# Stage-one blocks from GpSimd sums in a Fourier mixer and MLP on one NeuronCore

## The chip, the cores and the metric

One core of a Trainium2 chip runs the whole kernel in one launch. Its engines are TensorE (PE, with its weight loads shown as PEld), VectorE (DVE), ScalarE (ACT), GpSimd (POOL) and SyncE (SP), which here only issues DMAs. The metric is the device time of one execution in microseconds; the median of the runs counts.

## The reference

```python
B, S, D, FF = 8, 3008, 256, 2048            # batches, sequence, width, hidden width
X = np.fft.rfft(x, axis=1)                  # along the 3008 rows of each batch
Yr = X.real @ w_r - X.imag @ w_i + b_r
Yi = X.real @ w_i + X.imag @ w_r + b_i
Y = shrink(Yr, 0.01) + 1j * shrink(Yi, 0.01)   # sign(v) * max(|v| - 0.01, 0)
y = np.fft.irfft(Y, n=3008, axis=1).reshape(B * S, D)
out = np.maximum(y @ w_in, 0) ** 2 @ w_out  # 24064 tokens, 256 -> 2048 -> 256
```

## The kernel before

The transform over 3008 = 64 x 47 rows is done in two stages each way, by products with constant matrices. **Stage one** of a batch is 13 blocks (q = 0 to 12) of 120 partitions. A block is loaded as xt, which holds two halves of 2 x 256 columns; the host has laid row g beside its mirror row, so that the sum of the two halves goes through the cosine matrix am and their difference through the sine matrix. There are two ways to do a block. `Fwd` lets GpSimd make sum and difference (xs, two operations of line 215) and TensorE multiply each once (two products of line 236). `Fwd2` leaves GpSimd out: it multiplies both halves and lets the accumulator add them, with nam, the negative of the sine matrix, for the second half of the difference (four products of line 352). Either way ScalarE copies the result out of the accumulator psf into xe, and a DMA stores it to s in DRAM. **Stage two** (`Pair`, 12 a batch) reads two groups of all 13 blocks back (ka) with their matrices (kb), multiplies them (line 280), splits the result into a high and a low part (kxh by ScalarE, kxl by VectorE or GpSimd) and mixes it with the complex weights (line 301); shrink and the first inverse stage follow. The second inverse stage (`Back`: loads du, products of lines 461, 464 and 465, results yr) gives the tokens of the MLP.

**The MLP** runs in 48 tiles of 500 or 504 tokens (six to a batch), each in eight steps. A step does its first layer by seven products of half blocks, each as three passes of high and low parts (line 484, accumulators psh), in place of eight; VectorE puts the accumulators together (mp, mu, mv, mc), ScalarE applies relu and square and rounds to the high part of mg, GpSimd subtracts to get the low part, and TensorE multiplies by wout into pso. The operands of the seven products are sums of the tile's tokens (yt), made by VectorE for tile 0 and by GpSimd from tile 1 on. The MLP's weights come as 64-bit words in 16 parts; their conversion (dst, da, df, dw and then win or wout, lines 148 to 163) runs before the main part for 13 of them and for the last three inside it, at the half steps m = 1, 3 and 5 (`LATER`).

Batch 0 and blocks 0 to 4 of batch 1 (`PRE = 5`) are done in the front part. The main part then runs a loop over half steps m. In its first 16 the remaining eight blocks of batch 1, q = 5 to 12, are put between the steps of tile 0, at m of 0.5 + 0.9 (q - 5). The first `Pair` of batch 1 comes at 11.2, where tile 1's inverse stage is done too. Batch 2's blocks, by `Fwd`, start at 14.6.

What sets the order: the numbers beside each job give the order in which the program is recorded; a scheduler then orders each engine's instructions by its own model of times. `then` holds TensorE, VectorE, ScalarE and GpSimd to the recorded order for the steps' own operations, `load_next` does so for the loads on SP's queue. Tiles have 2 buffers where the tables say nothing; psf has two banks, xs, xe and du one buffer. The memory of the conversion is given up behind m = 5, and the tiles named in `SIDE` (xs among them) move there. nam is made twice, once for the front part and once for the main part (lines 712 and 713).

Of the kernel before, what the change touches and what calls it, by code (L numbers as in the profile page):

```python
# [9 lines left out]
F32 = mybir.dt.float32  # L10
# [13 lines left out]
B, S, D, FF = 8, 3008, 256, 2048  # L24
# [3 lines left out]
R, J = 5, 13  # L28
M1 = R * G
# [8 lines left out]
}  # L38
MAIN = {
    "xs": 1, "xe": 1, "du": 1, "kv": 1, "kp": 1, "kq": 1, "ksh": 1, "ksl": 1, "kxl": 1, "kb": 1, "yr": 1,  # L40
    "ms": 1, "mp": 1, "mu": 1, "mv": 1, "mc": 3, "nam": 1,
}
CONV = ("big", "small", "dw", "ds")
SIDE = ("xs", "ka", "kb", "kcm", "kxh", "kxl", "kp", "kq", "ke", "kv", "ksh", "ksl", "kuh", "kul", "ku")

# [11 lines left out]
def fnet_moe(ctx: ExitStack, tc, x, w_r, w_i, b_r, b_i, w_in, w_out, bm, cm, dx, a32, c32, out):  # L59
    nc = tc.nc  # L60
# [278 lines left out]
    class Fwd2(Fwd):  # L339
# [2 lines left out]
            with tc.issue_after(after.ins):  # L342
                nc.sync.dma_start(self.xt, x[self.b, :, self.q:self.q + 1])

        def add(self):
            pass

        def run(self):
            ps = bank([128, 2, D])
            for t in range(2):  # L350
                for i in range(2):
                    nc.tensor.matmul(
                        ps[:M1, t], nam if t and i else am32[:, t], self.xt[:, 0, i], start=i == 0, stop=i == 1
                    )
            self.ev = T("xe", [M1, 1, 2, D], F32, tag="xe" if self.q >= PRE else "xf")
            copy(act, self.ev[:, 0], ps[:M1])
            self.store(nc.sync if self.q >= PRE else act)

# [305 lines left out]
    PRE = 5  # L666
    nam = T("nam", [M1, M1], F32)
    act.mul(nam, am32[:, 1], -1.0)
    second = [Fwd2(1, q) for q in range(J)]
    for r in range(-5, len(units) + 3):  # L670
        at(units, r + 5, "load")
        at(units, r + 1, "fwd", "bins")
# [36 lines left out]
            chain[nc.sync] = p.get  # L709
    for n in range(len(parts) - LATE, min(LATER.values())):  # L710
        convert(n, units[-1])
    nam = T("nam", [M1, M1], F32)
    act.mul(nam, am32[:, 1], -1.0)
    for q in range(PRE, PRE + 2):
        second[q].load()
    jobs = []
    for m in range(2 * len(steps) + 4):
        b, r = divmod(m, slots)
        if r == 0 and b < B:
            jobs = [(t - slots, job) for t, job in jobs]  # L720
            if b + 1 < B:
                first, step, end = 1.0, 6.1, 7.1
                if b == 0:
                    first, step, end = 11.2, 5.3, 9.1
                    for q in range(PRE, J):
                        if q > PRE + 1:
                            jobs += [(0.9 * (q - PRE - 2), second[q].load)]
                        jobs += [(0.5 + 0.9 * (q - PRE), second[q].run)]
                    jobs += [(first - 0.6, pairs[1][0].load)]
                jobs += pair_tasks(pairs[b + 1], first, step, end)  # L730
            if b + 2 < B:
                first, step = (2.6, 7.0) if b else (14.6, 6.0)
                jobs += fwd_tasks(b + 2, first, step) + [(95.0, pairs[b + 2][0].load)]
            for j in range(len(HALF)):
                t = b * len(HALF) + j + 1
                if t < len(tiles):
                    jobs += back_tasks(t, NF * j + 0.5)
            jobs.sort(key=lambda j: j[0])
        n, k = divmod(m, 2)
        if k and 0 <= n - 2 < len(steps):  # L740
            steps[n - 2].out(1)
        if n < len(steps):
            (steps[n].second if k else steps[n].first)()
        if not k and 0 <= n - 2 < len(steps):
            steps[n - 2].out(0)
        if m in LATER:
            convert(LATER[m], steps[n])
        if m == max(LATER):
            conv.close()
            pools.update(dict.fromkeys(CONV), **dict.fromkeys(SIDE, memory(ctx, "side")))  # L750
        while jobs and jobs[0][0] < r + 1:
            jobs.pop(0)[1]()
# [86 lines left out]
```

## Time and profile before

| | us |
|---|---|
| runs of the kernel before | 2613.71, 2615.43, 2618.53 |
| their median | 2615.43 |
| the profiled execution | 2614.82 |
| its span in the trace | 2613.1 |
| TensorE busy in it | 2564.3 |
| VectorE, ScalarE, GpSimd busy | 1782.3, 1672.7, 1657.0 |

The profile gives one execution: the busy time of each engine, the same by stretches of time, each instruction with what ended the idle time ahead of it, and the waits that each engine had. A share over the whole span is an average of stages: the front part, where the weights are converted and batch 0 is transformed, ends at about 126 us; the change lies behind it.

### The profile page before, as it was taken

To read this page: it belongs to the slowest core of one execution; us is meant where nothing else is said; L and a number is where in the kernel's file an instruction comes from. 1 tells how busy PE (TensorE), PEld (TensorE's weight loads), DVE (VectorE), ACT (ScalarE), POOL (GpSimd) and SP (SyncE) were. 2 spreads that over 40 slices of the span, in tenths; PEclk is the share of its full clock that TensorE was granted. 3 is DMA by queue.
4 is the path that set the end of the run, shared out by engine and by line. 5 is a ranking of instruction groups with operands and counts; after the bars stand their busy time and mean duration, and the time that the engine had idled before them with its cause. 6 is when DMAs were issued, how large, how long until landed. Compare 5 with 4: busy or idle time off the path is not lost.

```text
span 2613.1 us, 47540 instructions
## 1 busy us (share of the span) xinstructions
PE 2564.3 (98%) x16908; PEld 2347.0 (90%) x16908; DVE 1782.3 (68%) x3797; ACT 1672.7 (64%) x2434; POOL 1657.0 (63%) x1628
## 2 busy tenths in 40 slices
PE   6799999999999999999999999999999999999999
PEld 4689989999999999999999999999999999999998
DVE  6877766667767767577676776667676677765554
ACT  3556656666666666666666666666666666666665
POOL 2246666766766667667666676666667666666564
PEclk8999999999999999999999999999999999999999
DMA  8733332333332332233332333323332223221100
GB/s 267 236 110 110 102 113 82 95 106 107 95 91 75 116 104 86 84 95 113 104 92 82 97 110 100 99 76 101 103 108 80 71 79 101 71 65 41 33 17 17
DMA packets 191455, 250.51 MB, mean 96 GB/s; under 512 B 21755, under 2 KB 135923, under 8 KB 191219
## 3 DMA queue, kind: packets, MB, share of 16 engines
q1 hardware_dynamic: 178240, 223.89, 28.1%
q0 software_dynamic: 12304, 22.35, 3.6%
q8 instruction: 136, 2.23, 0.4%
q10 hardware_dynamic: 675, 1.23, 0.2%
q14 instruction: 100, 0.82, 0.1%
HBM read 146.85 MB, written 100.53 MB: 95 GB/s over the span
## 4 chain that ended last, share of the span: by engine, by line
PE 84%; POOL 1%; DMA 1%; issue 0%; DVE 0%; ACT 0%; POOLq 0%; SPq 0%; ACTq 0%; DVEq 0%
PE pso L484 36%; PE psh L484 32%; PE psf L301 6%; PE psf L280 2%; PE psf L236 2%; PE psf L333 2%; PE psf L464 1%; PE psf L465 1%; PE psf L461 1%; DMA du<-s 1%; POOL mg L101 0%; POOL yt L101 0%; POOL ms L101 0%; POOL ms L500 0%; ACT mc L484 0%
## 5 line engine op out<-in xcount | busy, mean ns | idle before, releaser
L101 POOL TENSOR_TENSOR mg<-mc,mg 128x500 fp32r<-128x500 f32 (+1 forms) x768 | 975.0, 1290 | 594.3 <-ACT mg L97 549.7
L484 PE MATMUL pso<-mg,wout 128*128 128x500 f32 (+1 forms) x4608 | 1176.2, 392 | 1.8 <-ACT mg L97 1.3
L484 PE MATMUL psh<-yt,win 128*128 128x250 f32 (+1 forms) x8064 | 1072.9, 281 | 1.5 <-DVE mc L484 1.2
L484 ACT ACTIVATE mc<-mc 128x1000 f32<-128x1000 f32 (+1 forms) x768 | 802.6, 1045 | 406.6 <-DVE mc L484 397.3
L484 PEld LDWEIGHTS psh<-yt,win 128*128 128x128 f32 x8064 | 1022.2, 189 | 34.3 <-PE psh L484 1.9
L484 PEld LDWEIGHTS pso<-mg,wout 128*128 128x128 f32 x4608 | 818.7, 189 | 130.0 <-POOL mg L101 1.9
L484 DVE TENSOR_TENSOR mc<-psh,mv 128x500 f32<-128x500 f32 (+3 forms) x768 | 419.1, 547 | 428.1 <-PE psh L484 395.4
L97 ACT CAST mg<-mc 128x1000 fp32r<-128x1000 f32 (+1 forms) x384 | 396.9, 1034 | 18.4 <-ACT mc L484 0.4
L484 DVE TENSOR_TENSOR mv<-psh,mu 128x500 f32<-128x500 f32 (+1 forms) x384 | 260.6, 679 | 53.5 <-PE psh L484 21.8
L301 PE MATMUL psf<-wx,kxh 128*128 128x256 f32 x1008 | 206.7, 281 | 2.4 <-ACT kxh L97 1.7
L98 DVE COPY mp<-psh 128x250 f32<-128x250 f32 (+1 forms) x384 | 159.7, 416 | 39.2 <-PE psh L484 16.2
L301 PEld LDWEIGHTS psf<-wx,kxh 128*128 128x128 f32 x1008 | 166.3, 189 | 6.7 <-ACT kxh L97 1.9
L101 POOL TENSOR_TENSOR ksl<-kv,ksh 128x512 fp32r<-128x512 f32 x84 | 108.8, 1295 | 94.6 <-ACT ksh L97 94.5
L484 DVE TENSOR_TENSOR mu<-psh,mp 128x250 f32<-128x250 f32 (+1 forms) x384 | 160.5, 418 | 11.5
L215 POOL TENSOR_TENSOR xs<-xt 120x256 f32<-120x256 f32 x156 | 115.4, 760 | 72.5 <-DMA xt<-x_in 67.6
L484 DVE TENSOR_TENSOR mc<-psh,mp 128x250 f32<-128x250 f32 (+1 forms) x384 | 156.8, 408 | 4.3 <-PE psh L484 2.8
L322 DVE TENSOR_TENSOR kv<-psf,ke 64x256 f32<-64x256 f32 x336 | 141.8, 422 | 22.9 <-PE psf L301 14.2
L301 PE MATMUL psf<-wx,kxl 128*128 128x256 f32 x504 | 141.1, 280 | 1.0 <-DVE kxl L101 1.0
L97 ACT COPY dy<-psf 128x188 f32<-128x188 f32 x256 | 76.9, 313 | 82.7 <-PE psf L465 82.2
L313 DVE TENSOR_TENSOR ke<-psf,bias 128x512 f32<-128x512 f32 x84 | 58.0, 691 | 102.0 <-PE psf L301 101.9
L97 ACT CAST ksh<-kv 128x512 fp32r<-128x512 f32 x84 | 52.0, 619 | 114.3 <-DVE kv L101 113.4
L97 ACT CAST kuh<-psf 128x256 fp32r<-128x256 f32 x192 | 68.4, 372 | 88.2 <-PE psf L333 71.4
(102 smaller groups left out, 2565.4 us busy)
## 6 DMA issues: line engine op xcount, KB each, us to landing
du<-s SPq DMA_DIRECT2D x128, 256.0 KB, 2.9
s<-kuh SPq DMA_DIRECT2D x192, 128.0 KB, 1.8
s<-kul SPq DMA_DIRECT2D x192, 128.0 KB, 1.8
kcm<-cm_in POOLq DMA_DIRECT2D x84, 256.0 KB, 3.3
ka<-s SPq DMA_DIRECT2D x84, 256.0 KB, 3.4
s<-xe SPq DMA_DIRECT2D x87, 240.0 KB, 2.4
xt<-x_in SPq DMA_DIRECT2D x86, 240.0 KB, 3.3
du<-s SPq DMA_DIRECT2D x256, 64.0 KB, 2.8
```

What stands on the lines that cost most here:

```text
L97: return act.copy(out=out, in_=in_)
L98: return eng.tensor_copy(out=out, in_=in_)
L101: return eng.tensor_tensor(out=out, in0=a, in1=b, op=ALU.subtract)
L215: return eng.tensor_tensor(out=out[:, :n], in0=self.xt[:, :n, 0], in1=self.xt[:, :n, 1], op=(ALU.add, ALU.subtract)[t])
L236: nc.tensor.matmul(ps[:M1, t], am32[:, t], self.u[:, t], start=True, stop=True)
L280: nc.tensor.matmul(pv[:, :, c, g, :], self.a[:, g, c * 128:(c + 1) * 128], bg, start=True, stop=True)
L301: self.last = nc.tensor.matmul(ps, l, wx[j][:, k, c, :], start=n == 0, stop=n == 5)
L313: dve.tensor_add(out=self.e, in0=self.pe, in1=bias)
L322: dve.tensor_add(out=v[64 * r:64 * r + 64, g], in0=ps[gs], in1=self.e[gs, r])
L333: nc.tensor.matmul(ps[:, :D], self.cm[:, g, j * 128:(j + 1) * 128], r[:, g], start=n == 0, stop=n == 2)
L461: mm = nc.tensor.matmul(pv[:, :, 0], self.u[:, 0, cs], dx_sb[:, 0], start=True, stop=False)
L484: last_of[eng] = op(*args, **kwargs)
```

## The change

The eight blocks q = 5 to 12 of batch 1 are done by `Fwd` in place of `Fwd2`. Each gets a job `add` (two GpSimd operations, xs from xt) 0.6 of a half step ahead of its job `run`, which issues two products in place of four. The second nam and its ScalarE operation go; xs lies in the main memory from the start, and no longer in the one that is opened behind m = 5. The evacuation tile and the queue of the stores stay what they were for these blocks (xe, SP); `Fwd2`, now for the front part alone, loses the choice.

```diff
 MAIN = {
-    "ms": 1, "mp": 1, "mu": 1, "mv": 1, "mc": 3, "nam": 1,
+    "ms": 1, "mp": 1, "mu": 1, "mv": 1, "mc": 3,
 }
-SIDE = ("xs", "ka", "kb", "kcm", "kxh", "kxl", "kp", "kq", "ke", "kv", "ksh", "ksl", "kuh", "kul", "ku")
+SIDE = ("ka", "kb", "kcm", "kxh", "kxl", "kp", "kq", "ke", "kv", "ksh", "ksl", "kuh", "kul", "ku")
...
-        def add(self):
-            pass
-
         def run(self):
...
-            self.ev = T("xe", [M1, 1, 2, D], F32, tag="xe" if self.q >= PRE else "xf")
+            self.ev = T("xe", [M1, 1, 2, D], F32, tag="xf")
             copy(act, self.ev[:, 0], ps[:M1])
-            self.store(nc.sync if self.q >= PRE else act)
+            self.store(act)
...
-    second = [Fwd2(1, q) for q in range(J)]
+    second = [(Fwd2 if q < PRE else Fwd)(1, q) for q in range(J)]
...
-    nam = T("nam", [M1, M1], F32)
-    act.mul(nam, am32[:, 1], -1.0)
     for q in range(PRE, PRE + 2):
         second[q].load()
...
-                        jobs += [(0.5 + 0.9 * (q - PRE), second[q].run)]
+                        at = 0.5 + 0.9 * (q - PRE)
+                        jobs += [(at - 0.6, second[q].add), (at, second[q].run)]
```

The order of the instructions changes from the start of the main part up to about a quarter into the tokens of batch 1; behind that TensorE's rows are the same. Line numbers of the changed kernel are three lower from line 352 on (its line 481 is line 484 of before). Three places follow.

TensorE, the start of the main part, before: psh_1249 and psh_1250 are the first accumulators of tile 0's first step, yt_1197 and yt_1198 the high and low parts of its tokens, am_76 the stage-one matrix.

```order
L484 MATMUL psh_1249<-yt_1197,win_81 128x252
L484 MATMUL psh_1249<-yt_1197,win_82 128x252
L484 MATMUL psh_1249<-yt_1198,win_81 128x252
L352 MATMUL psf<-xt,am_76 120x256 x3
L352 MATMUL psf<-xt,nam 120x256
L352 MATMUL psf<-xt,am_76 120x256 x3
L352 MATMUL psf<-xt,nam 120x256
L484 MATMUL psh_1249<-yt_1197,win_81 128x252
L484 MATMUL psh_1249<-yt_1197,win_82 128x252
```

The same place with the change, where the first accumulator is psh_1247:

```order
L481 MATMUL psh_1247<-yt_1197,win_81 128x252
L481 MATMUL psh_1247<-yt_1197,win_82 128x252
L481 MATMUL psh_1247<-yt_1198,win_81 128x252
L236 MATMUL psf<-xs,am_76 120x256
L481 MATMUL psh_1247<-yt_1197,win_81 128x252
L481 MATMUL psh_1247<-yt_1197,win_82 128x252
L236 MATMUL psf<-xs,am_76 120x256
L481 MATMUL psh_1247<-yt_1198,win_81 128x252
```

Two blocks (eight products) stood between the accumulator's first and second product; one block (two products) stands there now, and the second block has moved behind.

GpSimd, the start of the main part, before: kul ends the front part, yr is tile 1's first piece, each mg pair is the low part of a half step.

```order
L101 TENSOR_TENSOR kul<-ku,kuh 128x256 x22
L477 COPY yr<-dy 128x2x60
L101 TENSOR_TENSOR mg_1301<-mc,mg_1300 128x504 x2
L101 TENSOR_TENSOR mg_1401<-mc,mg_1400 128x504 x2
L101 TENSOR_TENSOR yt_1681<-yr,yt_1680 128x252
L101 TENSOR_TENSOR mg_1506<-mc,mg_1505 128x504 x2
L101 TENSOR_TENSOR mg_1615<-mc,mg_1614 128x504 x2
```

The same place with the change:

```order
L101 TENSOR_TENSOR kul<-ku,kuh 128x256 x22
L215 TENSOR_TENSOR xs<-xt 120x256 x2
L474 COPY yr<-dy 128x2x60
L215 TENSOR_TENSOR xs<-xt 120x256 x4
L101 TENSOR_TENSOR mg_1303<-mc,mg_1302 128x504 x2
L215 TENSOR_TENSOR xs<-xt 120x256 x2
L101 TENSOR_TENSOR mg_1405<-mc,mg_1404 128x504 x2
L215 TENSOR_TENSOR xs<-xt 120x256 x2
L101 TENSOR_TENSOR mg_1512<-mc,mg_1511 128x504 x2
L215 TENSOR_TENSOR xs<-xt 120x256 x2
L101 TENSOR_TENSOR yt_1687<-yr,yt_1686 128x252
```

Three blocks' sums stand ahead of the first mg pair, and one block's behind each of the pairs that follow.

TensorE, the end of tile 0, before: line 280 is the first product group of batch 1's first `Pair`, and pso_1453 and pso_1454 are tile 0's output accumulators.

```order
L484 MATMUL psh_1834<-yt_1198,win_81 128x252
L280 MATMUL psf<-kb,ka 128x2x64 x4
L484 MATMUL pso_1453<-mg_1737,wout_83 128x504
L484 MATMUL pso_1453<-mg_1737,wout_84 128x504
L484 MATMUL pso_1454<-mg_1737,wout_83 128x504
L484 MATMUL pso_1454<-mg_1737,wout_84 128x504
```

And, 21 products further on, the start of tile 1's first step (psh_1924, from tile 1's tokens yt_1680 and yt_1681), before:

```order
L484 MATMUL psh_1924<-yt_1680,win_81 128x252
L484 MATMUL psh_1924<-yt_1680,win_82 128x252
L484 MATMUL psh_1924<-yt_1681,win_81 128x252
L484 MATMUL psh_1924<-yt_1680,win_81 128x252
L484 MATMUL psh_1924<-yt_1680,win_82 128x252
L301 MATMUL psf<-wx_79,kxh 128x256
L484 MATMUL psh_1924<-yt_1681,win_81 128x252
```

With the change (psh_1930 is that step's first accumulator):

```order
L481 MATMUL psh_1842<-yt_1198,win_81 128x252
L481 MATMUL psh_1930<-yt_1686,win_81 128x252
L481 MATMUL psh_1930<-yt_1686,win_82 128x252
L481 MATMUL psh_1930<-yt_1687,win_81 128x252
L280 MATMUL psf<-kb,ka 128x2x64 x4
L481 MATMUL psh_1930<-yt_1686,win_81 128x252
L481 MATMUL psh_1930<-yt_1686,win_82 128x252
L301 MATMUL psf<-wx_79,kxh 128x256
L301 MATMUL psf<-wx_79,kxl 128x256
L301 MATMUL psf<-wx_80,kxh 128x256
```

Line 280 has moved behind tile 1's first three products, and line 301 follows it by two products in place of 26. Block 12's two products stand 37 rows ahead of line 280 (25 of psh, 12 of pso).

## Rows read from the trace of the kernel before

**Rows 1.** The page: busy time, share of the span and instructions of each engine.

```profile
PE 2564.3 (98%) x16908; PEld 2347.0 (90%) x16908; DVE 1782.3 (68%) x3797; ACT 1672.7 (64%) x2434; POOL 1657.0 (63%) x1628
```

**Rows 2.** Busy us by stretch (from:to, length, engines), granted clock, DMA share, GB/s.

```profile
130.00:135.00 5.00, 4.37 (x10) 3.39 (x11) 0.60 (x1) 0.59 (x1) 0.01 (x1) 0.50 0.05 14
...
140.00:150.00 10.00, 10.00 (x60) 8.92 (x59) 9.44 (x18) 8.16 (x12) 2.92 (x3) 1.00 0.51 143
150.00:160.00 10.00, 9.86 (x62) 8.63 (x61) 10.00 (x19) 5.99 (x11) 3.08 (x3) 1.00 0.26 70
160.00:170.00 10.00, 9.59 (x62) 8.66 (x61) 9.72 (x20) 6.38 (x10) 6.37 (x6) 1.00 0.39 113
...
350.00:360.00 10.00, 7.73 (x53) 6.92 (x52) 5.15 (x12) 6.40 (x11) 10.00 (x13) 1.00 0.21 63
```

**Rows 3.** TensorE's waits, 110 to 420 us: for whom; total us, times, longest.

```profile
PE psf L352 <- DVE yt L101: 3.3, 1, 3.3
PE psf L461 <- DVE yr L471: 2.6, 1, 2.6
```

**Rows 4.** Timeline of VectorE (start, us, instruction, [idle before, releaser]): the first copy.

```profile
136.85 0.42 DVE L98 COPY mp<-psh 128x252 f32<-128x252 f32 x1 [6.25 <-PE psh L484]
```

**Rows 5.** Timeline of TensorE: two blocks at full clock.

```profile
141.65 1.46 PE L352 MATMUL psf<-xt,am 120*120 120x256 f32 x6
...
143.37 1.46 PE L352 MATMUL psf<-xt,am 120*120 120x256 f32 x6
```

**Rows 6.** Timeline of TensorE: the start of the main part.

```profile
126.46 0.90 PE L484 MATMUL psh<-yt,win 128*128 128x252 f32 x3
130.63 2.89 PE L352 MATMUL psf<-xt,am 120*120 120x256 f32 x6 [3.27 <-DVE yt L101]
133.31 1.06 PE L352 MATMUL psf<-xt,nam 120*120 120x256 f32 x2
```

**Rows 7.** Tile xs, GpSimd: durations in ns (min, median, max), first and last start.

```profile
L215 POOL TENSOR_TENSOR xs<-xt x156: 717/739/1219, 183.4 to 2009.9; 120x256 f32<-120x256 f32 x156
```

**Rows 8.** VectorE by line and shape, 137 to 170 us (busy us, mean ns | idle before); tile df.

```profile
L484 DVE TENSOR_TENSOR mv<-psh,mu 128x504 f32<-128x504 f32 x5 | 3.4, 679 | 0.3
...
L152 DVE SCALAR_TENSOR_TENSOR df<-da,df 128x512 int32<-128x512 int32 x3 | 3.2, 1055 | 0.0
...
L101 DVE TENSOR_TENSOR wout<-dw,wout 128x512 fp32r<-128x512 f32 x2 | 2.2, 1082 | 0.0
...
L152 DVE SCALAR_TENSOR_TENSOR df<-da,df x16: 673/683/1647, 28.1 to 163.3; 128x512 int32<-128x512 int32 x16
```

**Rows 9.** Timeline of TensorE: behind block 12, and line 280 to line 301.

```profile
174.10 0.59 PE L352 MATMUL psf<-xt,nam 120*120 120x256 f32 x2
174.34 1.86 PE L484 MATMUL psh<-yt,win 128*128 128x252 f32 x13
...
181.92 1.05 PE L280 MATMUL psf<-kb,ka 128*128 128x128 f32 x8
182.73 2.99 PE L484 MATMUL pso<-mg,wout 128*128 128x504 f32 x12
185.55 1.81 PE L484 MATMUL psh<-yt,win 128*128 128x252 f32 x14
187.20 0.28 PE L301 MATMUL psf<-wx,kxh 128*128 128x256 f32 x1
```

**Rows 10.** Timeline of SP's queue: block 12's store, and the loads behind it.

```profile
175.34 0.32 SPq L225 DMA_DIRECT2D s<-xe  x1
177.86 0.39 SPq L108 DMA_DIRECT2D ka<-s  x1
178.34 0.42 SPq L108 DMA_DIRECT2D kb<-bm_in  x1
```

**Rows 11.** The page, DMA issues: count, KB each, us from issue to landing.

```profile
ka<-s SPq DMA_DIRECT2D x84, 256.0 KB, 3.4
```

**Rows 12.** Timelines of ScalarE and VectorE: the first Pair's split.

```profile
183.69 0.59 ACT L97 CAST kxh<-psf 128x512 fp32r<-128x512 f32 x1
...
184.32 0.69 DVE L101 TENSOR_TENSOR kxl<-psf,kxh 128x512 fp32r<-128x512 f32 x1 [0.62 <-ACT kxh L97]
```

## The prediction

> **What bounds the kernel now.** First the table of busy times: TensorE is busy for 98% of the span, no other engine over 68% [rows 1]. So over the whole run a product taken from TensorE is worth its time. But the change acts between 130 and 190 us only, so the second view is the busy time by stretch [rows 2]. There a different picture stands: between 140 and 170 us TensorE is busy 29.45 of 30 us and VectorE 29.16 of 30, because the last three weight conversions lie there beside the seven products' sums. In this stage two engines are full at once, and taking work from one of them leaves the other as the bound. Third, the waits of TensorE [rows 3]: the longest of the stretch from 110 to 420 us is 3.3 us, ahead of the first of the eight blocks (put down to a VectorE sum; in TensorE's order the next work is block 5's products, which need the block's load, so that load landed at about 130.6). Fourth, what follows it: the block's products run at a granted clock of 0.50, the 1.2 GHz level, after that idle stretch [rows 2], and the first accumulators of tile 0's first step come only behind two whole blocks. VectorE stands idle for 6.25 us until then and starts its copy at 136.85 [rows 4].
>
> **The change part by part.** *Products.* Eight blocks lose two products each. At full clock a block of four takes 143.37 − 141.65 = 1.72 us [rows 5], so 0.43 a product; 16 products are 6.9 us of TensorE's time. At the half clock three products take 133.31 − 130.63 = 2.68, so 0.89 each [rows 6].
>
> *The start.* Block 5's two products now need two sums first. A sum of this shape takes 0.74 us on GpSimd [rows 7], and the next product waits only for the first one: TensorE goes on at 130.6 + 0.75 = 131.4 and not at 130.63, which loses 0.8. But the new order (first pair of fences ahead) puts one block of two products, not two blocks of four, among the first six psh products. Up to the first accumulator: 131.4 + 2 × 0.89 + 0.90 (three psh products at this clock [rows 6]) = 134.1. VectorE's copy starts at 134.1 in place of 136.85: **−2.8**, and VectorE is what bounds from here on.
>
> *140 to 170 us.* Six of the eight blocks lie here. The change takes nothing from VectorE, so what TensorE saves beyond the start only turns into waits of TensorE. The start's gain is kept, less three things. (a) VectorE now starts earlier than its inputs are spread, so a few early accumulators are waited for: the fifth psh accumulator and ScalarE's part of the first conversion, 0.8 by the order (bounds 0 and 2): **+0.8**. (b) Ten GpSimd sums run beside conversion steps, and the two disturb each other. The conversion step at line 152 takes 1.06 us in the mean of its three runs in this stage and 0.68 in the median of its 16 [rows 8], the three meeting GpSimd's work; a VectorE sum that reads PSUM takes 0.68 in the same stage and does not stretch [rows 8]. So only a conversion step that meets a sum is stretched, and GpSimd's sums mostly stand between its mg subtractions, where VectorE works from PSUM. The price of one meeting lies between nothing and the whole sum of 0.75, ten of them 0 to 7.5. I take two short meetings of 0.3, nearest to the 0.37 by which line 152 is stretched: **+0.6**. (c) One wout subtraction (1.08 us [rows 8]) falls behind step 3's out products in the new order; half of it lay where VectorE had to wait anyway: **−0.6**. So the out products of step 3 come 2.8 − 0.8 − 0.6 + 0.6 = 2.0 us earlier.
>
> On (b) the Trainium skill has a rule that speaks against this change. The page "SBUF — State Buffer", section "Who interferes with whom", says that VectorE and GpSimd share one pair of ports under an exclusive lock, which an operation holds for its whole length, VectorE's share of it being taken by operations with two SBUF inputs. By it every sum that meets a conversion step would hold that step up for its whole 0.75. The trace agrees that SBUF-only steps are stretched and PSUM-reading ones are not; how often they meet, no row of before can show.
>
> *Behind 170 us.* Before, one block of four products was left here (1.72); in the new order two blocks of two (2 × 0.86): 0. Two halves of an inverse stage two, three products each (lines 461, 464 and 465), stood ahead of the point up to which the 2.0 us count and stand behind it in the new order: six products at 0.11, a little under the 0.12 from one psh product to the next [rows 9]: **+0.65**.
>
> *Tile 1's first step.* Here the new order costs. Block 12 is the last of the eight; its evacuation is stored, and the store is read back by the first Pair of the second batch (ka) with kb behind it on the same queue. Before: the block's products end at 174.34 [rows 9], the store is issued at 175.34 and kb at 178.34 [rows 10], and a transfer of the ka kind takes 3.4 [rows 11], so line 280 can begin at some 181.5: 7.2 after the block. It began at 181.92 without a wait [rows 9]. In the new order (third pair of fences) 25 psh and 12 pso products stand between the block and line 280: 25 × 1.65/14 + 2.82 = 5.8 us [rows 9]. So TensorE waits 7.2 − 5.8 = 1.4: **+1.4**. Behind line 280 there stood 12 pso and 14 psh products before line 301 (5.3 us from 181.92 to 187.20); now two psh products stand there. But line 301 needs kxh of ScalarE, cast from 183.69 to 184.28, and its second product kxl of VectorE, done at 185.0 [rows 12]: 2.4 and 3.1 us behind the start of line 280. That instruction takes 0.8, the psh products 0.24: a wait of 1.3 to 2.05. I take **+1.4**, since both engines had other work ahead of these steps before. Queued behind the waiting TensorE is all of tile 1's step, and VectorE, ScalarE and GpSimd wait with it.
>
> *The rest.* One ScalarE operation (nam) less: no wait of the trace hangs on it, nothing. The store of the eight blocks stays on SP. The side pool gives xs up to the main one, so xs has one buffer from the start: the sum of a block waits for both products of the block before, and the queue behind it on GpSimd (mg) waits too; priced in (a). Behind line 301 and up to some 520 us the order differs in small pieces; afterwards it is the same. The largest pocket there, with TensorE busy for 7.73 of 10 us [rows 2], holds the same sequence before and after, so it stays.
>
> Sum: −2.0 + 0.65 + 1.4 + 1.4 = **+1.45** on the profiled execution's 2614.82, which is 2616.3. The median of the runs is 0.6 above that execution; with a part of that, **2616.5**.
>
> **Rivals.** *One: TensorE bounds all through.* If VectorE catches up (the conversions' last steps wait for nothing and slide behind), each saved product counts: −6.9 + 0.8 for the first sum = −6.1, and no wait at line 280: 2608.7, faster. For it: TensorE at 98% [rows 1], and 29.45 of 30 in the stage itself. Against it: VectorE's 29.16 of 30 beside that [rows 2].
>
> *Two, on the other side: the sums hold VectorE up.* The place is 140 to 170 us, the mechanism the meeting of sums and conversion steps. At the whole price ten sums cost 7.5 in place of 0.6: 2616.5 + 6.9 = 2623.4. It ends beyond 2620.7 (0.2% over the median of before) from 4.8 us on, that is from some six sums at 0.75. For it: the 1.06 against 0.68 of line 152 [rows 8]. Against it: GpSimd's sums stand next to mg, which fits into VectorE's PSUM work. It is this case that the rule of the Trainium skill's page "SBUF — State Buffer" gives.
>
> *Three: no new wait at tile 1's first step.* If blocks 11 and 12 run earlier than the order suggests, the 2.8 us fall away: 2613.7. For it: GpSimd has much idle time here. Against it: one xs buffer, so the eight blocks go one at a time.
>
> **How the numbers follow.** My forecast 0.45, rival one 0.17, rival two 0.21, rival three 0.17. About 0.2% (5.2 us) is what a measurement of this kernel can tell from no change. Faster is rival one: 0.17. Same is the forecast and rival three: 0.62. Slower is rival two: 0.21. The range reaches to both outer cases, 2608.7 and 2623.4, and half a microsecond beyond: 2608 to 2624. What is left out is the further ends of rivals one and two, under 2 in 10. The forecast's own range is 2613 to 2620 (bounds of (a) and of the wait at line 301).
>
> **What would show it.** Start: VectorE's first mp copy at about 134.1 and 131.4 for TensorE's first product. Stage: VectorE still full from 140 to 170 while TensorE's busy time falls by some 4 us; if TensorE stays full, rival one. Line 152 at a mean over 1.4 us would be rival two. Tile 1: a wait of 1 to 2 us each at lines 280 and 301, near 183 to 187; no such rows would be rival three. Behind 520 us all slices are alike, only shifted. The prediction is wrong if the eight blocks end up waiting for their loads or their single xs buffer, so that TensorE stands idle between 134 and 170 by more than the products saved, or if the pocket at 350 to 363 us goes or grows.

## The result and the profile after

| | before | after |
|---|---|---|
| median of 17 runs each, us | 2616.97 | 2622.42 |
| ratio, with its 95% interval | | 1.0019 (1.0011 to 1.0026) |
| the profiled execution, us | 2614.82 | 2622.51 |
| its span, us | 2613.1 | 2620.7 |

The change made the kernel 5 us slower, 0.19%: the interval leaves 1 out, and the size is just under the 0.2% that the prediction took as the least that can be told from no change. One of the 17 runs of the changed kernel took 3150.95 us at a granted clock of 0.75, and the ratio goes by the other 16. The forecast was 2616.5 with a range of 2608 to 2624: the time lies in the range, 5.9 us above the forecast. A second set of runs gave a ratio of 1.0011 (1.0002 to 1.0020), which is 3 us.

The page of the changed kernel, the busy time of each engine (answers [rows 1]):

```profile
PE 2562.2 (98%) x16876; PEld 2342.3 (89%) x16876; DVE 1792.7 (68%) x3797; ACT 1673.3 (64%) x2433; POOL 1669.7 (64%) x1644
```

TensorE has less work and the span is longer, so TensorE waits more. Where, the busy time by stretch shows (columns as in [rows 2]):

```profile
140.00:150.00 10.00, 9.58 (x64) 8.52 (x64) 9.47 (x18) 7.34 (x11) 8.52 (x8) 1.00 0.40 116
150.00:160.00 10.00, 7.07 (x43) 6.08 (x43) 10.00 (x19) 7.29 (x11) 6.90 (x6) 1.00 0.33 97
160.00:170.00 10.00, 9.48 (x47) 8.28 (x48) 10.00 (x19) 5.35 (x7) 7.29 (x9) 0.83 0.31 89
```

In the stage of the eight blocks VectorE is as full as it was (29.47 of 30 us, 29.16 before), and TensorE fell from 29.45 to 26.13. Behind its waits there TensorE's granted clock was 0.83 from 160 to 170 us, where it was 1.00 before; the run xs2 below separates this from VectorE's part.

Timelines of the changed kernel: TensorE at the start of the main part (answers [rows 6]), VectorE's first copy [rows 4], TensorE at tile 1's first step [rows 9], and SP's queue ahead of it [rows 10]:

```profile
127.47 0.90 PE L481 MATMUL psh<-yt,win 128*128 128x252 f32 x3
132.77 1.21 PE L236 MATMUL psf<-xs,am 120*120 120x256 f32 x2 [4.39 <-POOL xs L215]
```

```profile
135.50 0.42 DVE L98 COPY mp<-psh 128x252 f32<-128x252 f32 x1 [3.87 <-PE psh L481]
```

```profile
179.97 0.60 PE L236 MATMUL psf<-xs,am 120*120 120x256 f32 x2
180.22 1.85 PE L481 MATMUL psh<-yt,win 128*128 128x252 f32 x13
...
186.86 1.13 PE L280 MATMUL psf<-kb,ka 128*128 128x128 f32 x8 [0.64 <-DMA kb<-bm_in]
187.74 0.48 PE L481 MATMUL psh<-yt,win 128*128 128x252 f32 x2
188.94 0.38 PE L301 MATMUL psf<-wx,kxh 128*128 128x256 f32 x1 [0.71 <-ACT kxh L97]
189.66 0.38 PE L301 MATMUL psf<-wx,kxl 128*128 128x256 f32 x1 [0.34 <-DVE kxl L101]
```

```profile
184.18 0.42 SPq L108 DMA_DIRECT2D kb<-bm_in  x1
```

The front part of this execution is 1.0 us later than in the one before it (127.47 against 126.46 for the same three products), with the same order of TensorE; in the eleven executions (before and ten of the table below) that have the conversions in the main part they start between 124.7 and 127.5, so that is scatter. The comparison is therefore made from the first psh product on. The table gives, for the out products that begin a step (counted in groups of 12), how much later (+) or earlier (−) than in the first execution of before they start, each counted from its own first psh product. The out products of step 3 are those at 170 us, and tile 1's first step lies between those at 183 and at 190 us. The table is worked out from rows of the timelines such as these, of before and after in that order:

```profile
169.81 1.54 PE L484 MATMUL pso<-mg,wout 128*128 128x504 f32 x6
...
190.30 2.91 PE L484 MATMUL pso<-mg,wout 128*128 128x504 f32 x12
```

```profile
169.14 2.21 PE L481 MATMUL pso<-mg,wout 128*128 128x504 f32 x9
...
192.72 2.44 PE L481 MATMUL pso<-mg,wout 128*128 128x504 f32 x10
```

| out products, at (before, us) | 146 | 163 | 170 | 183 | 190 | 322 | 367 | 469 | 489 | end |
|---|---|---|---|---|---|---|---|---|---|---|
| after | −4.4 | −3.1 | −1.7 | −1.8 | +1.4 | +0.5 | +3.9 | +7.7 | +6.4 | +6.6 |
| after_again | −4.6 | −3.8 | −2.0 | −2.2 | +1.2 | +0.4 | +4.2 | +7.7 | +6.5 | +5.4 |
| before_again | +0.2 | −0.2 | −0.2 | −0.2 | −0.2 | −0.3 | +3.6 | +3.7 | +3.7 | +3.8 |
| products_only | −3.4 | −2.1 | −1.8 | −3.5 | −2.7 | −4.0 | −2.6 | −2.7 | −2.8 | −3.1 |
| sums_only | +0.1 | +2.0 | +2.2 | +2.2 | +2.2 | +2.2 | +6.0 | +6.4 | +6.4 | +6.4 |
| xs2 | −3.4 | −1.9 | −0.5 | −2.2 | −1.4 | −2.7 | −2.0 | −2.1 | −2.2 | +1.3 |
| pocket_q8 | −0.2 | −0.5 | −0.5 | −0.5 | −0.5 | −0.5 | +2.4 | +3.5 | +3.5 | +2.4 |
| store_act | −3.7 | −2.6 | −1.1 | −1.3 | +2.2 | +1.5 | +5.4 | +5.4 | +5.7 | +6.2 |
| before_spread_c | −0.2 | −0.8 | −0.7 | +2.4 | +1.0 | +2.3 | +2.5 | +3.1 | +3.1 | +2.8 |
| xs2_spread_c | −3.6 | −6.2 | −6.1 | −2.7 | −1.2 | −1.6 | −0.1 | +0.1 | 0.0 | +4.2 |
| conv_early_before | +0.2 | −1.5 | −1.0 | −2.0 | −2.1 | −2.9 | 0.0 | −0.1 | −0.1 | −0.6 |
| conv_early_after | +0.7 | −1.7 | −1.8 | −3.3 | −2.8 | −4.7 | −3.6 | −3.7 | −3.7 | −4.5 |
| conv_early_xs2 | +3.6 | −0.1 | −0.5 | −1.5 | −1.6 | −2.4 | 0.0 | −0.2 | −0.2 | +4.3 |

### The profile page after: what moved, and what is told of

Its sections match the earlier page's. It is cut to its first block, busy times and chain, and to the rows that moved or that the text cites. A ratio compares the mean times of both kernels' runs of the same rounds, so it can differ in the third digit from the quotient of the medians.

```text
span 2620.7 us, 47499 instructions
## 1 busy us (share of the span) xinstructions
PE 2562.2 (98%) x16876; PEld 2342.3 (89%) x16876; DVE 1792.7 (68%) x3797; ACT 1673.3 (64%) x2433; POOL 1669.7 (64%) x1644
## 4 chain that ended last, share of the span: by engine, by line
PE 89%; DVE 3%; DMA 3%; POOL 3%; issue 1%; ACT 1%; SPq 0%; POOLq 0%; ACTq 0%; DVEq 0%
PE pso L481 38%; PE psh L481 34%; PE psf L301 7%; PE psf L280 3%; PE psf L236 3%; PE psf L333 2%; POOL mg L101 1%; PE psf L461 1%; PE psf L462 1%; PE psf L458 1%; PE psf L412 1%; DMA du<-s 1%; DMA s<-xe 0%; DMA x<-x_in 0%; DMA s<-kuh 0%
## 5 line engine op out<-in xcount | busy, mean ns | idle before, releaser
L215 POOL TENSOR_TENSOR xs<-xt 120x256 f32<-120x256 f32 x172 | 129.2, 771 | 113.4 <-DMA xt<-x_in 100.6
```

The source lines that it names most:

```text
L215: return eng.tensor_tensor(out=out[:, :n], in0=self.xt[:, :n, 0], in1=self.xt[:, :n, 1], op=(ALU.add, ALU.subtract)[t])
```

## The experiments

**The same two kernels again.** The theory after the first trace was that the losses lie in the new order of instructions (order); its rivals were that GpSimd's sums are the cost wherever they stand (sums), and that chance meetings of VectorE and GpSimd operations make the difference (meeting). No edit:

> The changed kernel a second time. In the first trace it lost, against before and counted from the first psh product: it gained 4.4 us up to the first out products, kept 1.7 of them at step 3's out products, stood 1.4 behind at tile 1's first step, 3.9 behind after the pocket at 355 to 372 us (a wait of 4.4 us at line 301 against 1.7) and 6.6 at the end. If the losses lie in the order (theory order), the second trace shows the same ledger within half a microsecond at each place, and a time 5 us over before. If some are chance meetings of VectorE and GpSimd operations (theory meeting), the waits at the pocket differ between the two traces by 2 us or more while the instruction order is the same.

> The kernel before a second time. Theory order: the waits of the first trace, 1.7 us at line 301 in the pocket at 355 to 367 us and no wait at tile 1's first step, come again within half a microsecond. Theory meeting: the pocket's wait differs by 1 us or more.

Measured: 2619.41 us in the median (1.0011, 1.0002 to 1.0020) for the changed kernel, 2617.5 for one run of before. In the table the two executions of the changed kernel agree within 0.7 us at each place up to 489 us, and store_act below, which has the same order of TensorE up to 447 us, lies 0.6 to 1.0 us above them from 170 to 322 us, with the same step from 170 to 190 us (3.1, 3.2 and 3.3 us). So the ledger comes again with the order to about a microsecond, not to the half that was expected, and the time is 3 us over before and not 5. The two executions of before agree within 0.25 us up to 322 us and then part: the pocket at 355 to 367 us is 3.9 us longer in the second. TensorE's waits between 340 and 380 us, before, and from 110 to 420 us, before_again:

```profile
PE psf L301 <- ACT kxh L97: 1.7, 1, 1.7
```

```profile
PE psf L301 <- ACT kxh L97: 5.7, 1, 5.7
```

The order is the same to the last row on all four engines. VectorE's and GpSimd's rows in the pocket show what differs: before, then before_again.

```profile
359.09 0.93 DVE L324 TENSOR_SCALAR kc<-kv 128x512 f32<-128x512 f32 x1
...
360.39 0.77 DVE L101 TENSOR_TENSOR kv<-kv,kc 128x512 f32<-128x512 f32 x1
...
359.68 0.92 POOL L215 TENSOR_TENSOR xs<-xt 120x256 f32<-120x256 f32 x1
360.55 0.57 POOL L108 DMA_DIRECT2D kcm<-cm_in  x1
361.15 2.45 POOL L101 TENSOR_TENSOR mg<-mc,mg 128x500 fp32r<-128x500 f32 x2
```

```profile
357.76 4.56 DVE L324 TENSOR_SCALAR kc<-kv 128x512 f32<-128x512 f32 x1
...
358.24 2.44 POOL L101 TENSOR_TENSOR mg<-mc,mg 128x500 fp32r<-128x500 f32 x2
360.63 0.38 POOL L477 COPY yr<-dy 128x248 f32<-128x248 f32 x1
360.98 1.06 POOL L101 TENSOR_TENSOR yt<-ms,yt 128x500 fp32r<-128x500 f32 x1
```

In the first, kc got between two of GpSimd's operations and took 0.93 us; in the second it took 4.56 us and ended at 362.32, 0.3 us after GpSimd's unbroken run of operations (360.98 + 1.06 = 362.04). ksh, kxh and then line 301 wait behind it. So meeting holds for the pocket in the kernel before. Between the two executions of the changed kernel the wait at line 301 there differs by 1.4 us (4.4 and 5.8), under the 2 that theory meeting asked for. For the rest the ledger goes with the order.

**Products without sums, sums without the saving.** The first leaves the sums out of the eight blocks, so their stage one is not computed; the second makes sums that nobody reads.

```diff
+    class FwdP(Fwd):
+        def add(self):
+            pass
+        def run(self):
+            self.u = self.xt[:, 0]
+            super().run()
...
-    second = [(Fwd2 if q < PRE else Fwd)(1, q) for q in range(J)]
+    second = [(Fwd2 if q < PRE else FwdP)(1, q) for q in range(J)]
```

> The eight blocks with two products each, straight from the two halves of xt; the sums by GpSimd are left out, so the second batch's stage one is not computed for these blocks. Theory sums (GpSimd's sums hold VectorE's conversions up and delay the first product): without them the conversion steps at lines 151 to 163 are as short as before, the gain at step 3's out products is 4 us and not 1.7, and the kernel is 3 to 6 us faster than before. Theory order (the loss lies at tile 1's first step and behind, where line 280 has moved): the gain up to step 3 is lost there all the same, 0 to 3 us slower than before. Had TensorE bounded all through: 6.9 us faster.

```diff
-SIDE = ("xs", "ka", ...
+SIDE = ("ka", ...
...
         def add(self):
-            pass
+            if self.q >= PRE:
+                super().add()
...
-                        jobs += [(0.5 + 0.9 * (q - PRE), second[q].run)]
+                        at = 0.5 + 0.9 * (q - PRE)
+                        jobs += [(at - 0.6, second[q].add), (at, second[q].run)]
```

> The eight blocks keep their four products on xt, and GpSimd makes the 16 sums beside them, which nobody reads. Theory sums: the conversion steps stretch, step 3's out products come 2 to 4 us later than before, and the kernel is 2 to 6 us slower. Theory order: GpSimd has idle time here, within 1.5 us of before.

Measured: products_only 2610.09 us, 0.9977 (0.9967 to 0.9986), 6 us faster than before; sums_only 2618.71, 1.0005 (0.9996 to 1.0014). The time of products_only is what theory sums expected, and not the 0 to 3 us slower of theory order. At step 3's out products (170 us), where theory sums expected 4 us to be left without sums, 1.8 were left, as with them (1.1 to 2.0). So most of the saving goes in the stage without any sum, with VectorE busy for 28.59 of 30 us from 140 to 170 also here.

The kernel sums_only has the order of before to the last row on TensorE, VectorE and ScalarE, so it prices the sums alone. Put beside four products they cost 2.2 us at step 3's out products, within the 2 to 4 of theory sums, and nothing more up to the pocket. By its time, 1.0005 with that interval, the 2 to 6 us of theory sums cannot be told from the 1.5 of theory order. VectorE's rows agree: its 25 conversion steps in the main part took 19.1 us in before and 18.7 in before_again, 19.3 in products_only, 20.5 in both executions of the changed kernel and 21.1 in sums_only. The sums do have a price in the stage, 1 to 2 us, beside what VectorE's fullness takes.

The difference of the two two-product kernels opens at tile 1's first step (−3.5 to −2.7 without sums, −1.8 to +1.4 with them). There line 280 stands 221 rows of psh and pso into the main part without sums, 219 before, and 243 in the changed kernel. It reads what the last of the eight blocks stores, and that block stands 172 rows in without sums and 206 in the changed kernel: line 280 has moved with it. The pocket of products_only lies between the two executions of before (−4.0 to −2.6, so 1.4 us over the first): kc took 0.59 us there and the subtraction behind it 2.86.

**Two buffers for xs.** One number:

```diff
-    "xs": 1, "xe": 1, "du": 1, ...
+    "xs": 2, "xe": 1, "du": 1, ...
```

> The changed kernel with two buffers for xs in place of one; nothing else is edited. The order that follows has line 280 at 223 rows of psh and pso, line 301 at 245, as the kernel with products alone has and nearly as before (219, 245); in the changed kernel they stand at 243 and 245. Theory order: the loss at tile 1's first step (3.2 us from step 5's to step 6's out products in the changed kernel) goes to under 0.5, the gain of about 2 us up to there is kept, and the kernel is 3 to 7 us faster than the changed one, at or below before. Theory sums (what GpSimd does is the cost, wherever it stands): the 16 sums are still made, so it is no more than 1 us faster than the changed kernel.

Measured: 2615.96 us, 0.9996 of before (0.9987 to 1.0004), which is the changed kernel's loss undone but no gain. The step into tile 1 costs 0.8 us and not 3.2 (−2.2 to −1.4), with all 16 sums still made: most of that loss is the order's and not the sums', though 0.8 is over the 0.5 that was expected. Most of the saving is lost in the stage again (0.5 us left at 170 us). TensorE's granted clock is 1.00 in all three stretches from 140 to 170 us here, and VectorE is busy for 30.00 of 30, so the loss in the stage does not need the lower clock that the changed kernel has there:

```profile
150.00:160.00 10.00, 5.90 (x36) 4.86 (x35) 10.00 (x19) 6.23 (x10) 6.03 (x5) 1.00 0.27 75
```

The 2.1 us that it holds at 489 us go further on, 0.5 to 1.2 us in each of five batches: the second buffer changes the order in the later batches as well, and a wait of TensorE stands there that before does not have. Waits of TensorE from 600 to 2600 us:

```profile
PE psf L333 <- ACT ksh L97: 3.0, 5, 0.8
```

**The pocket with a shorter run of GpSimd.** The kernel before, with one block of batch 2 multiplied straight from xt (its sum and difference are left out):

```diff
         def add(self):
+            if (self.b, self.q) == (2, 8):
+                self.u = self.xt[:, 0]
+                return
             self.u = T("xs", [M1, 2, D], F32)
```

> The kernel before with one block of the third batch (the one whose two GpSimd sums stand in the pocket at 355 us) done by two products straight on xt; its sum and difference are left out of the computation. GpSimd's unbroken run of operations beside the pocket gets 1.4 us shorter. Theory meeting (VectorE's kc at line 324 is held until GpSimd's run ends: 4.56 us where it lost, 0.93 where it won): kc takes at most 3.2 us or under 1, the pocket is 1 to 3.6 us shorter than in its long form, and the kernel's time is 0.5 to 3 us under before. If GpSimd is not the cause, kc takes 4.5 us again and the time is that of before.

Measured: 2616.74 us, 1.0000 (0.9991 to 1.0009). kc took 3.50 us, 1.1 less than in before_again and 0.3 over the bound set for theory meeting. The two sums that are left out were over before kc began in before_again, so they are not what it waited for. What was left of GpSimd's run when kc began is 3.2 us (361.28 − 358.07) and not 4.3 (362.04 − 357.76): yr's copy, 0.4 us, moved ahead of mg, and kc began later beside the run.

```profile
358.07 3.50 DVE L327 TENSOR_SCALAR kc<-kv 128x512 f32<-128x512 f32 x1
...
357.82 2.44 POOL L101 TENSOR_TENSOR mg<-mc,mg 128x500 fp32r<-128x500 f32 x2
360.22 1.06 POOL L101 TENSOR_TENSOR yt<-ms,yt 128x500 fp32r<-128x500 f32 x1
```

It ended at 361.57, 0.3 after GpSimd's run (361.28), as in before_again. The length of the hold follows what is left of the run. That the pocket costs less on average is not shown: the time is that of before, 0.5 to 3 us under it were expected, and how often the kernel before has the short pocket of its first execution stays open.

**Stores on another queue.** The changed kernel, with the stores of batch 2's blocks issued by ScalarE:

```diff
-            self.store()
+            self.store(act if self.b == 2 else nc.sync)
```

> The changed kernel with the stores of the third batch's stage-one blocks issued on ScalarE's queue and not on SP's; TensorE's order is the same to the last row. In the changed kernel one such store stands on SP for 10 us, from 455.6 to 465.6, ahead of the du loads of tile 2's next pieces, and TensorE then waits 2.5 us in all at lines 458 to 462 near 473. Theory queue: the du loads are issued some 10 us earlier, that wait goes to under 0.5, and the kernel is 1 to 3 us faster than the changed one. If the wait has another cause (the psf bank, or ScalarE's copy of dy), it stays at 2 us or more. ScalarE's 13 issues may cost up to half a microsecond each in its own queue.

(The tile meant is tile 6, the first of batch 1's tokens. TensorE's order is the same for its first 1900 rows only, up to some 440 us, not to the last row.) Measured: 2618.00 us, 1.0003 of before (0.9994 to 1.0013). The wait is gone: from 322 to 489 us the ledger has +1.5, +5.4, +5.4, +5.7, where the changed kernel rises by 2.5 more behind the pocket. The profiled execution ends at +6.2 all the same, since it stood 1.5 higher at the pocket's end, and the intervals of 1.0003 and of the changed kernel's 1.0011 overlap, so a faster kernel is not shown. And the reason given is wrong. The du loads were issued as late as before, since the ka load in front of them on SP waits for that very store. The changed kernel, then store_act:

```profile
465.63 0.34 SPq L225 DMA_DIRECT2D s<-xe  x1
468.03 0.38 SPq L108 DMA_DIRECT2D ka<-s  x1
...
469.57 6.70 SPq L108 DMA_DIRECT2D du<-s  x4
...
472.64 0.47 PE L481 MATMUL psh<-yt,win 128*128 128x252 f32 x2
474.24 0.36 PE L458 MATMUL psf<-dx_sb,du 128*128 128x188 f32 x1 [1.13 <-DMA du<-s]
```

```profile
469.14 1.46 SPq L108 DMA_DIRECT2D du<-s  x3
...
473.35 1.07 PE L481 MATMUL pso<-mg,wout 128*128 128x500 f32 x4
474.25 0.25 PE L458 MATMUL psf<-dx_sb,du 128*128 128x188 f32 x1
```

Counted from the first psh product, line 458 runs 348.8 us on in store_act and 346.8 in the changed kernel, so no earlier; but store_act's order has the psh products and four out products in front of it, the changed kernel's two psh products and then nothing. In before the block behind that store ran at 453.7, its store went at 455.36, and the du loads at 459.36. In the changed kernel that block ran at 463.95, ten us later: 4.4 of them are the delay so far (1.0 of the front part and 3.4 in the ledger), the other 5.8 its later place in the order. So the chain is: the last block of batch 2 later in the order, its store, ka, du behind ka on one queue, and an order of TensorE that does not allow for it.

**The conversions spread or moved.** If VectorE bounds the stage, its load there is what to change. The kernel before, the kernel xs2, and the changed one, with

```diff
-    LATER = {1: 13, 3: 14, 5: 15}
+    LATER = {1: 13, 5: 14, 9: 15}
```

for spread_c. For conv_early all three go into the loop ahead of the main part:

```diff
-    LATER = {1: 13, 3: 14, 5: 15}
+    LATER = {5: 16}
...
-        if m in LATER:
-            convert(LATER[m], steps[n])
```

> The kernel before with the last three conversions at half steps 1, 5 and 9 in place of 1, 3 and 5. VectorE's load is spread over a longer stretch, but TensorE was nearly full there with four products a block: theory VectorE-bound expects no more than 1.5 us either way.

> The changed kernel with two xs buffers and the last three conversions at half steps 1, 5 and 9. Theory VectorE-bound: with VectorE's load spread, the two-product blocks keep 2 to 4 us more of their saving up to step 3's out products than with xs2 alone (0.5 us kept there), and the kernel is 2 to 6 us faster than before. If the stage is held by the blocks themselves, it is as xs2, within 1 us of before.

Measured: before_spread_c 2617.23 us, 1.0000 (0.9991 to 1.0009); xs2_spread_c 2617.95, 1.0004 (0.9995 to 1.0013). Up to step 3's out products the theory holds: −6.1 with two products a block, where xs2 has −0.5 with nothing but the place of the conversions changed, and −0.7 with four products. Seven blocks stand ahead of that place in both, so 14 products are saved, 6.0 us at 0.43; 5.4 of them show. TensorE is nearly full there again (29.63 of 30 us), and VectorE has some room (27.95; 8.22 of the last 10):

```profile
140.00:150.00 10.00, 10.00 (x61) 8.91 (x60) 9.97 (x16) 5.81 (x9) 9.85 (x9) 1.00 0.53 154
150.00:160.00 10.00, 9.63 (x58) 8.44 (x57) 9.76 (x20) 8.78 (x12) 6.77 (x7) 1.00 0.22 65
160.00:170.00 10.00, 10.00 (x66) 9.03 (x66) 8.22 (x17) 6.63 (x11) 7.98 (x7) 1.00 0.13 40
```

That xs2_spread_c would be 2 to 6 us faster than before was wrong. The third conversion now meets tile 1's token sums on GpSimd, and TensorE waits for mu behind it; the gain of 6.7 us is down to 2.7 twelve products later, and before_spread_c loses 2.9 at the same place:

```profile
175.44 3.02 PE L481 MATMUL psh<-yt,win 128*128 128x252 f32 x12 [2.69 <-DVE mu L481]
...
171.97 1.43 DVE L159 SCALAR_TENSOR_TENSOR dw<-dst,da 128x512 f32<-128x512 uint32 x1
...
173.65 1.41 DVE L163 TENSOR_TENSOR dw<-dw,df 128x512 f32<-128x512 f32 x1
174.98 0.41 DVE L481 TENSOR_TENSOR mu<-psh,mp 128x252 f32<-128x252 f32 x1
...
172.81 1.70 POOL L101 TENSOR_TENSOR yt<-ms,yt 128x504 fp32r<-128x504 f32 x1
```

> The kernel before with the last three weight conversions made ahead of the main part and not in its first half steps; beside conv_early_after. VectorE then has only the steps' sums in the stage of the eight blocks. The stretch from the first psh product to the out products of step 3 took 43.35 us before. Theory VectorE-bound (the conversions fill VectorE, so saved products only become waits): TensorE bounds here instead, and the stretch is its own work alone, about that of before since TensorE was nearly full there, 38 to 44 us. The kernel as a whole is later by the conversions' time ahead of the main part, some 10 us.

> The changed kernel with the last three weight conversions made ahead of the main part. Against conv_early_before. Theory VectorE-bound: without the conversions the saved products count, and the stretch from the first psh product to step 3's out products is shorter by 4 to 7 us (the changed kernel against before, with the conversions inside: 1.7 to 2.0). If the stage is held by the blocks themselves (loads, the single xs buffer, the sums on GpSimd), it is shorter by no more than 2.5 us here as well.

> The changed kernel with two xs buffers and the last three conversions ahead of the main part. With one buffer and the early conversions the first psh accumulator waited 7 us in pieces for the blocks (sums, xs, du) at the half clock, and by step 3's out products only 0.7 us were left of the 6.9 us of saved products. Theory (VectorE bounds the stage with the conversions in it, the single buffer without them): with both out of the way the stretch from the first psh product to step 3's out products is 3 to 6 us shorter than in conv_early_before, no new wait stands at tile 1's first step since line 280 stands at 186 rows, and the kernel is 3 to 8 us faster than before. If the stage's waits come from elsewhere, it is within 2 us of conv_early_after's stretch and 1 to 4 us faster than before.

Measured, of one run each: conv_early_before 2618.3 us, conv_early_after 2612.7, beside a before of 2616.89; conv_early_xs2 2622.10 in the median, 1.0021 (1.0012 to 1.0030). The stretch to step 3's out products is 42.3, 41.6 and 42.8 us: none of the 4 to 7 (or 3 to 6) us that were expected. Nor was conv_early_before some 10 us later, but 1.4 in its one run, and conv_early_xs2 is 5 us slower and not 3 to 8 faster. The edit does not do what it was meant to do: the scheduler puts the conversions between the token sums of tile 0, so that VectorE delivers tile 0's operands late, and TensorE waits for them, at a granted clock of 0.50 to 0.69 from 130 to 145 us in conv_early_xs2. Its rows, TensorE, then VectorE:

```profile
139.08 0.79 PE L481 MATMUL psh<-yt,win 128*128 128x252 f32 x2 [3.37 <-ACT yt L97]
...
136.17 0.68 DVE L152 SCALAR_TENSOR_TENSOR df<-da,df 128x512 int32<-128x512 int32 x1
136.78 0.67 DVE L101 TENSOR_TENSOR yt<-ms,yt 128x504 fp32r<-128x504 f32 x1
137.37 0.68 DVE L159 SCALAR_TENSOR_TENSOR dw<-dst,da 128x512 f32<-128x512 uint32 x1
```

So these three tell nothing against VectorE as the bound, and nothing for it. Of conv_early_after's 4 us against before there is one run only; that it beats both kernels is not shown.

## Why the prediction was right, and where not

**The start.** A gain of 2.8 us at VectorE's first copy was forecast; it is 2.4 (135.50 − 127.47 = 8.0 against 136.85 − 126.46 = 10.4), and 2.7 in after_again. The first product waits 1.1 us longer than before, not 0.8. The load landed 4.0 us after the first psh product in both kernels; but the first sum began 0.5 us after the landing, where TensorE's product had begun 0.1 after it, and it took 0.72. As forecast, the product waited for that first sum alone. Right, a little too large.

**The stage.** 2.0 us were to be left at step 3's out products; 1.7 and 2.0 were, and 1.1 in store_act. The reason given, that VectorE is full and the saved products turn into waits, is borne out from both sides: products_only has 1.8 there without any sum, and xs2_spread_c keeps 5.6 more than xs2 once VectorE has room. (Five of the eight blocks lie between 140 and 170 us in the rows of before, not the six of the prediction; no term of its sum rests on that count.) That the number came out so well is in part luck: the start gave 0.4 less than forecast, the sums cost more, and the other terms made up for it. The price of sums meeting conversion steps had been taken as 0.6 between 0 and 7.5. By line and shape, the conversion steps of the changed kernel from 137 to 170 us, of which

```profile
L163 DVE TENSOR_TENSOR dw<-dw,df 128x512 f32<-128x512 f32 x3 | 3.7, 1236 | 0.0
...
L152 DVE SCALAR_TENSOR_TENSOR df<-da,df 128x512 int32<-128x512 int32 x3 | 2.5, 839 | 0.0
```

took 20.5 us together, against 19.1 before: 1.4 more, which is what two of the sums take and not ten; alone, in sums_only, they cost 2.2. The term was sized at less than half. Line 152, by which rival two would be known, is shorter than before (0.84 against 1.06 us [rows 8]) and was too narrow a sign, since the stretch fell on other lines (line 163, 1.24 us against 0.68 before). Rival two, at 6.9 us over the forecast by every sum at its full price, did not come about in this stage. Of the rule of the Trainium skill beside it (page "SBUF — State Buffer", section "Who interferes with whom") the trace agrees that operations from SBUF to SBUF are stretched and sums that read PSUM are not (0.68 us before and after); that every sum would meet one did not come out.

**Tile 1's first step.** 0.65 + 1.4 + 1.4 = 3.45 us were forecast from step 3 on; the ledger goes from −1.7 to +1.4 and from −2.0 to +1.2, 3.1 and 3.2. The waits stand where they were said to stand: 0.64 us at line 280 for kb, 0.71 and 0.34 at line 301 for kxh and kxl. They are smaller than 1.4 each: from block 12's products (180.22) to line 280 (186.86) it took 6.6 us and not 7.2, since line 280 began 2.7 us after kb's issue, where the prediction had taken the 3.4 of a ka load for it; and line 301 began 2.1 us after line 280 and not 2.4, since ScalarE stood idle when line 280's result came, where before two other operations stood ahead of it. So the waits were over-priced by 1.1 us (1.7 in all against 2.8), and what else moves behind the mark was under-priced by 0.8 (1.4 against 0.65). At this point the sum was +1.45, and +1.4 was measured, two errors of opposite sign.

**Two steps failed after it.** "Behind line 301 and up to some 520 us the order differs in small pieces" was priced at nothing. One of these pieces gives 1.0 us back near 285 us, where a wait of TensorE for mc is gone; another, the last block of batch 2 later in the order, costs 2.5 and 2.3 us at tile 6's first step in the two executions of the changed kernel. And "the largest pocket there holds the same sequence before and after, so it stays" took the same sequence for the same time. The pocket has a short and a long form, 3.9 us apart, in the kernel before with one and the same order. The one trace that the prediction rested on had the short one; the two of the changed kernel are 3.4 and 3.8 us over it (kc 4.66 us in the second; in the first 2.13, with 2.83 for the subtraction behind it). The prediction had named a pocket that grows as a sign of being wrong, and by that sign this step was wrong.

The account of the profiled difference of 7.6 us of span is then 1.0 of the front part, 0.45 up to 322 us (the 1.45 of the forecast less the 1.0 that comes back), 3.4 of the pocket's form, 2.5 of tile 6's first step and 0.25 in the rest. Against before in its long form only 1.6 us are left (5.4 − 3.8, second executions), which fits medians 3 to 5 us apart if before falls into the short form part of the time. That share is an assumption that fits, and no run shows it.

Of the outcomes, "same" was the forecast's own and rival three's with 0.62, and the measured 0.19% lies just within it; the direction of the forecast, a little slower, was right, its size (1.45 against 3 and 5 us) too small. In time, 2622.42 is beyond the forecast's own 2613 to 2620, and beyond the 2620.7 from which the prediction had rival two begin. The range holds it because it reached out to rival two, whose mechanism is not what made the time longer: so the hit is in part luck. Rival one, 2608.7, has almost the time of products_only (2610.1), but not its mechanism: 1.8 us and not all were left at step 3's out products there. Rival three did not occur.

## What to carry to other kernels

Where two engines are full in a stage, work taken from one of them buys little until the other has room (14 saved products showed 5.4 us with room, and with the start's gain 0.5 to 2.0 without): read the busy time of the stage, not of the span, and look for what else fills the second engine. A block that ends later moves everything that reads it, so walk through the new order until it is equal to the old one, and price each place where a consumer moved close behind its load. And look at a second execution before you take a wait in one trace for a constant of the kernel.

## What the runs showed of the hardware

A VectorE operation from SBUF to SBUF (kc, 0.59 us in products_only) was held for up to 4.66 us when GpSimd had several operations in a row: it ended 0.3 us after the last of them, in before_again and in pocket_q8 alike. The Trainium skill's page "SBUF — State Buffer", section "Who interferes with whom", has the engine that comes second blocked for the whole of one instruction; here the hold went over a row of them. The fourteen traces show when it gets in. In the seven in which kc starts 0.7 us or more ahead of the first of the two mg subtractions it takes 0.48 to 2.13 us (before: 359.09 against 361.15, 0.93 us). In the seven in which it starts 0.6 us ahead or less, or behind, it takes 3.50 to 4.66 us and ends 0.3 us after the run (before_again: 357.76 against 358.24, 4.56 us). So a few tenths of a microsecond decide over 4 us; what makes them differ between executions of one order is not shown.

TensorE's clock fell to the 1.2 GHz level after these waits: the mean granted clock was 0.51 of full speed from 360 to 370 us in before_again, and 0.83 in before. Whether this adds to the pocket's price is not shown, since the wait at line 301 alone is 4.0 us longer and the pocket 3.9:

```profile
360.00:370.00 10.00, 4.96 (x22) 4.66 (x23) 5.84 (x8) 1.78 (x4) 4.03 (x5) 0.51 0.32 94
```
